# Windowed attention and a soft mixture of experts: groups of 64 queries by eight heads, a masked copy of 32 columns, and the copy of the flipped x on VectorE

## The chip, the cores and the metric

The kernel runs on one core of a Trainium2 chip. The metric is device time in microseconds (us) of one execution. Engines are named as the profile names them: PE is TensorE (PEld its weight loads), DVE is VectorE, ACT is ScalarE, POOL is GpSimd, and SP is the engine that issues most of the transfers. TensorE writes its results into accumulators (the tiles whose names begin with `ps`, `s4`, `pq`, `xp`), which VectorE and ScalarE read; GpSimd works on the core's main memory alone.

## The reference

```python
B, H, S, D = 8, 8, 576, 64
scores = q @ k.T / 8                                   # per batch row and head
rel = pos[:, None] - pos[None, :]
bias = -2.0 ** -(h + 1) * abs(rel)
scores = where((rel >= 0) & (rel < 128), scores + bias, -1e9)
attn = softmax(scores)                                 # over keys
x = (attn @ v) as [B * S, H * D] = [4608, 512]         # all heads of a token side by side
logits = x @ phi                                       # [4608, 32], 8 experts of 4 slots
d = softmax(logits, over tokens); slot_input = d.T @ x # [32, 512]
slot_out[e] = relu(slot_input[e] @ w1[e]) @ w2[e]
out = softmax(logits, over slots) @ slot_out           # [4608, 512]
```

Each query sees its own key and the 127 before it.

## The kernel before

A batch row of 576 queries is cut into tiles of 128 queries, `t` = 0 to 3, and a tail of 64, `t` = 4. A **group** is what goes through the softmax at once: 128 partitions by four pieces of 128 keys. For `t` below 4 a group is 128 queries by four heads (`g` = 0, 1), for `t` = 4 it is 64 queries by eight heads. There are 9 groups a batch row and 72 in all, and the loop `for i in range(n)` (from L777) makes one turn for each.

**Scores** (`scores`, L237). A strip of 32 queries sees a window of 160 keys, five blocks of 32. TensorE first writes the bias ramp into a window of the accumulator with a small product (L259), then adds queries times keys (L266), 8 and 16 products of 32 rows by 160 columns. Tile 0 has no tile before it; there two ramp products (L247) and four products (L252) of 128 by 128 do.

**Masked copy** (`merge`, L274). The window of a strip begins at column 32 r, so that the oldest keys lie in the first 128 columns and the own keys in the second. The copy lays the one over the other under a triangular mask, so that each query has just 128 places: four pieces of 128 by 128 for `t` = 1 to 3 (L281), four of 64 columns for the tail (L283). For tile 0 it writes -1e30 over the keys that are still to come (L279).

**Softmax** (`softmax_front`, L330, and `expo`, L351). On VectorE one turn runs: masked copy of the new group, row maximum (L301), reciprocal of the old group's sums (L313, for which GpSimd's L309 prepares the sums), the scaled maximum (L304), normalisation of the old group (L317). Between them stand "fillers" of the expert routing. ScalarE then takes four exponentials with their sums (L357).

**Values**. Three turns later TensorE flips the attention (`flip`, L372) into the accumulator `pq`, ScalarE copies it out (`split`, L379), and GpSimd selects from it the part for the tile's own keys and the part for the tile before (L381 and L383, for the tail L386 and L388). A turn after that TensorE multiplies with V (`values`, L410): for `t` = 1 to 3 eight products with 128 queries, for tile 0 four, for the tail 16 with 64 queries. The profile shows each product of this precision as two records. ScalarE copies the finished x of a tile out (`x_store`, L426).

**Flipped x**. Each tile of x, two of the rows' tails together, is flipped by TensorE (`x_flip`, L438) into the other half of the banks of `pq`, and copied out (`x_keep`, L447, 128 partitions by 512). Four tiles make a pass: logits (L456), softmax over tokens and slots, and the running sum of slot inputs (L514).

What each engine does is written out by hand in program order: `do` notes an action for a later turn at one of four places (`pre`, `pe`, `act`, `dve`), `run` plays it. `x_flip` is noted for the place `pe`, at the end of a turn, behind the scores of the next group; `x_keep` for the place `act` of the turn after, behind the split and ahead of the product with V. On an engine the order of the program is kept.

After the last group a section written out by hand finishes the last four groups and the routing (L806 to L893, some 213 to 230 us of the span), and then the experts run (from L997): a stream of products with weights that are loaded meanwhile.

Of the kernel before, what the change touches and what calls it, by code (L numbers as in the profile page):

```python
# [23 lines left out]
NS = E * SPE  # L24
# [11 lines left out]
WIN = P + KB  # L36
NB = S // KB
HW = 512
CW = P + TAIL + NS
WARM = 6  # L40
# [28 lines left out]
def tile_attn_softmoe(  # L69
# [20 lines left out]
    mask_u = cst[:, 0:P].bitcast(I32)  # L90
    mask_t = cst[:, P:P + TAIL].bitcast(I32)
# [14 lines left out]
    ramp = cpool.tile([P, 2, 2, WIN], BF16, name="ramp")  # L106
# [4 lines left out]
    qs = [kq[:, NB * P + 2 * P * i:NB * P + 2 * P * i + 2 * P] for i in range(3)]  # L111
# [61 lines left out]
    def load_q(i, eng=None):  # L173
        b, t, g = groups[i]
        o = 4 * P * t + 2 * P * g
        (eng or nc.sync).dma_start(qs[i % 3], qd[b, :, o:o + 2 * P])
# [29 lines left out]
    with tc.manual_schedule(engines=ORDERED):  # L206
# [6 lines left out]
        nc.gpsimd.memset(cst[:, 0:P], 1.0)  # L213
        nc.gpsimd.affine_select(cst[:, 0:P], cst[:, 0:P], [[1, P]], ALU.is_gt, 0.0, base=0, channel_multiplier=-1)
# [17 lines left out]
        nc.scalar.dma_start(cst[:, P:], cstd)  # L232
# [4 lines left out]
    def scores(i):  # L237
        b, t, g = groups[i]
        s4 = s4s[i % 2]
        parts = [s4[:, 0:2], s4[:, 2:4]]  # L240
        if i == 0:
            parts = [ps_1.tile([P, 2, 2 * P], F32, tag="xp", name="s4_0"), pq[:, 0].rearrange("p (u w) -> p u w", u=2)]
            parts = parts[::-1]
        qt = qs[i % 3].rearrange("p (j w) -> p j w", w=width(t))
        if t == 0:
            for par, rows in enumerate(half):
                nc.tensor.matmul(  # L247
                    parts[par][:, :, 0:P], lhsT=ones[rows], rhs=ramp[rows, g, :, 0:P],
                    start=True, stop=False)
            for jj in range(2):  # L250
                for par, rows in enumerate(half):
                    nc.tensor.matmul(  # L252
                        parts[par][:, jj, 0:P], lhsT=qt[rows, jj], rhs=kall[rows, 0:4, 2 * g + jj],
                        start=False, stop=(jj == 1))
        else:
            strips = [(c // 2, c % 2) if t == 4 else (g, c) for c in range(4)]
            for par, rows in enumerate(half):
                for c, (h, r) in enumerate(strips):
                    nc.tensor.matmul(  # L259
                        s4[32 * c:32 * c + 32, 2 * par:2 * par + 2, 32 * r:32 * r + WIN],  # L260
                        lhsT=ones[rows, 0:32], rhs=ramp[rows, h], start=True, stop=False)
            for jj in range(2):
                for par, rows in enumerate(half):
                    for c, (h, r) in enumerate(strips):
                        m0 = 4 * (t - 1) + r
                        nc.tensor.matmul(  # L266
                            s4[32 * c:32 * c + 32, 2 * par + jj, 32 * r:32 * r + WIN],
                            lhsT=qt[rows, 2 * h + jj if t == 4 else jj, 32 * r:32 * r + 32],
                            rhs=kall[rows, m0:m0 + 5, 2 * h + jj], start=False, stop=(jj == 1))
        st[groups[i]] = {"s4": s4, "parts": parts}  # L270

    ALL, LO, HI = slice(0, 4), slice(0, 2), slice(2, 4)

    def merge(key, us=ALL):  # L274
        t = key[1]
        s4 = st[key]["s4"]
        if t == 0:
            m = len(range(4)[us])
            nc.vector.copy_predicated(merged(key, us), bc(mask_u, 1, m), bc(low, 1, m).to_broadcast([P, m, P]))  # L279
        elif t < 4:  # L280
            nc.vector.copy_predicated(s4[:, :, P:2 * P], bc(mask_u, 1, 4), s4[:, :, 0:P])  # L281
# [841 lines left out]
```

## Time and profile before

| | us |
|---|---|
| median of 3 runs (lowest to highest) | 289.14 (288.57 to 290.88) |
| the profiled execution | 288.49 |
| its span, first to last instruction | 286.0 |
| TensorE busy | 253.9 |
| VectorE busy | 221.6 |
| ScalarE busy | 205.6 |
| GpSimd busy | 112.9 |

The prediction's lines are from that one execution. A row of groups gives line, engine, operation, output and inputs, shapes, count, then busy us and mean ns of one, then the idle time of the engine just ahead of them and what ended it. The chain of waits follows the work that ended last back to its releasers; its pieces show start, length, engine, tile, line and, behind x, the records in it. Pieces of a chain are shorter than the rows' means, since one instruction begins before the one ahead of it has quite ended. A row of windows gives the stretch, its length, the busy time (and instructions) of PE, PEld, DVE, ACT and POOL, then the granted clock of TensorE, the share of the transfer engines and GB/s. Matmul ends are modelled, so that a busy TensorE is not one at its peak.

### The profile page before, as it was taken

How to read it: one execution, taken by the hardware profiler on the slowest of the kernel's cores; microseconds unless marked ns; L12 is line 12 of the kernel's file. 1: busy time of each engine (PE TensorE's matmuls, PEld its weight loads, DVE VectorE, ACT ScalarE, POOL GpSimd, SP SyncE). 2: the span in 40 equal slices, each digit the busy share in tenths (PEclk: the TensorE clock that was granted, in tenths of full speed). 3: DMA queues.
4: the chain of work that ended last, by engine and by line, in shares of the span. 5: the costliest groups of instructions: out<-in, count | busy, mean ns of one | idle time of the engine just before them, and what ended most of it. 6: DMA issues, size and time to landing. Idle time of an engine off the chain costs nothing.

```text
span 286.0 us, 13588 instructions
## 1 busy us (share of the span) xinstructions
PE 253.9 (89%) x5535; PEld 178.9 (63%) x5535; DVE 221.6 (77%) x509; ACT 205.6 (72%) x817; POOL 112.9 (39%) x218
## 2 busy tenths in 40 slices
PE   8588999799979889989979998998979899999990
PEld 4366676676757567667657765766756443687750
DVE  2889989998997999988998998798973352656451
ACT  2888889988888988998898988888783411044460
POOL 2044626662573276257527725466552011000000
PEclk9689999999999999999999999999999999999997
DMA  6645368869885987969797978866574579998997
GB/s 184 218 134 164 100 197 270 276 195 289 285 271 152 305 297 233 278 224 305 218 286 242 328 236 251 278 204 219 165 265 140 169 254 365 411 393 322 362 384 282
DMA packets 36754, 72.61 MB, mean 254 GB/s; under 512 B 4402, under 2 KB 15316, under 8 KB 36692
## 3 DMA queue, kind: packets, MB, share of 16 engines
q1 hardware_dynamic: 35972, 71.24, 75.7%
q8 instruction: 43, 0.70, 1.0%
q10 hardware_dynamic: 720, 0.51, 0.6%
q14 instruction: 19, 0.16, 0.2%
HBM read 62.29 MB, written 9.44 MB: 251 GB/s over the span
## 4 chain that ended last, share of the span: by engine, by line
PE 45%; DVE 23%; ACT 16%; POOL 7%; issue 5%; DMA 2%; DVEq 0%; ACTq 0%; POOLq 0%
ACT area L357 9%; PE xp L410 7%; DVE area L317 6%; DVE s L301 6%; PE s L266 5%; PE op L967 5%; PE hp L930 5%; PE po L992 4%; DVE s L281 3%; POOL area L381 3%; PE pq L372 3%; PE lp L456 2%; DVE s L279 2%; PE s L259 2%; ACT area L379 2%
## 5 line engine op out<-in xcount | busy, mean ns | idle before, releaser
L357 ACT ACTIVATE area<-s,nb 128x128 f32<-128x128 f32 x286 | 102.7, 391 | 13.8 <-DVE nb L304 10.4
L410 PE MATMUL xp<-area 128*64 128x128 f32 (+1 forms) x1104 | 74.5, 272 | 8.4 <-POOL area L381 5.3
L357 ACT ACTIVATION_READ_ACCUMULATOR area<-s,nb 128x1 f32 x286 | 65.4, 229 | 0.0
L410 PEld LDWEIGHTS xp<-area 128*64 128x64 f32 x1104 | 54.1, 137 | 18.0 <-POOL area L381 6.1
L317 DVE TENSOR_TENSOR area<-area,rs 128x512 f32<-128x512 f32 (+1 forms) x73 | 61.0, 836 | 1.6
L301 DVE TENSOR_REDUCE s<-s 128x4 f32<-128x512 f32 x71 | 49.5, 697 | 2.2
L379 ACT COPY area<-pq 128x512 f32<-128x512 f32 (+1 forms) x72 | 43.5, 605 | 10.7 <-PE pq L372 9.0
L266 PE MATMUL s<-kq 64*32 64x160 f32 x1792 | 43.8, 302 | 2.3 <-issue 2.3
L309 POOL TENSOR_SCALAR rs<-sm 128x4 f32<-128x4 f32 x70 | 15.0, 214 | 73.0 <-ACT area L357 71.6
L383 POOL TENSOR_SCALAR_AFFINE_SELECT area<-area 128x512 f32<-128x512 f32 x48 | 41.7, 870 | 3.3
L381 POOL TENSOR_SCALAR_AFFINE_SELECT area<-area 128x512 f32<-128x512 f32 x48 | 35.5, 740 | 15.5 <-ACT area L379 14.6
L281 DVE COPY_PREDICATED s<-cst,s 128x512 f32<-128x512 int32 x48 | 33.1, 689 | 6.1 <-PE s L266 5.6
L372 PE MATMUL pq<-unit_r,area 64*128 64x64 f32 x552 | 31.3, 233 | 3.7 <-ACT area L322 2.8
L266 PEld LDWEIGHTS s<-kq 64*32 64x32 f32 x1792 | 30.1, 107 | 4.1 <-issue 3.5
L372 PEld LDWEIGHTS pq<-unit_r,area 64*128 64x128 f32 x552 | 23.3, 140 | 11.8 <-issue 3.2
L259 PE MATMUL s<-ramp,ones 64*32 64x320 bf16 x448 | 18.7, 311 | 4.8 <-ACT area L357 4.5
L426 ACT COPY area<-xp 128x512 f32<-128x512 f32 (+1 forms) x37 | 21.4, 578 | 0.2
L447 ACT COPY area<-pq 128x512 f32<-128x512 f32 x34 | 20.7, 608 | 0.3 <-PE pq L432 0.3
L438 PEld LDWEIGHTS pq<-unit_r,area 64*128 64x128 f32 x264 | 11.1, 137 | 12.8 <-issue 9.7
L994 ACT COPY ob<-po 128x512 f32<-128x512 f32 x19 | 10.4, 591 | 11.4 <-PE po L992 11.4
L994 DVE COPY ob<-po 128x512 f32<-128x512 f32 x17 | 11.2, 686 | 6.6 <-PE po L992 6.5
L438 PE MATMUL pq<-unit_r,area 64*128 64x64 f32 x264 | 15.2, 233 | 0.9 <-ACT area L379 0.6
(173 smaller groups left out, 329.1 us busy)
## 6 DMA issues: line engine op xcount, KB each, us to landing
w<-w SPq DMA_DIRECT2D x53, 512.0 KB, 5.5
out<-ob SPq DMA_DIRECT2D x36, 256.0 KB, 3.9
kq<-q_t SPq DMA_DIRECT2D x69, 128.0 KB, 3.5
kq<-k_t SPq DMA_DIRECT2D x32, 256.0 KB, 3.9
area<-v_n SPq DMA_DIRECT2D x31, 256.0 KB, 4.2
area<-w SPq DMA_DIRECT2D x8, 512.0 KB, 4.6
area<-v_n SPq DMA_DIRECT2D x12, 128.0 KB, 4.4
kq<-w SPq DMA_DIRECT2D x3, 512.0 KB, 5.9
```

What stands on the lines that cost most here:

```text
L259: nc.tensor.matmul(s4[32 * c:32 * c + 32, 2 * par:2 * par + 2, 32 * r:32 * r + WIN], lhsT=ones[rows, 0:32], rhs=ramp[rows, h], start=True, ...
L266: nc.tensor.matmul(s4[32 * c:32 * c + 32, 2 * par + jj, 32 * r:32 * r + WIN], lhsT=qt[rows, 2 * h + jj if t == 4 else jj, 32 * r:32 * r + 32],
L281: nc.vector.copy_predicated(s4[:, :, P:2 * P], bc(mask_u, 1, 4), s4[:, :, 0:P])
L301: nc.vector.tensor_reduce(st[key]["mx"][:, us], merged(key, us), axis=AX.X, op=ALU.max, negate=True)
L317: nc.vector.tensor_tensor(p4, p4, bc(rs, 2, P), op=ALU.mult)
L357: nc.scalar.activation(s["p4"][:, u], merged(key, u), AF.Exp, bias=s["nb"][:, u:u + 1], scale=SCALE, accum_out=s["sm"][:, u:u + 1],)
L372: nc.tensor.transpose(s["pt"][:, u, r], s["p4"][rows, u], ident[rows, rows])
L379: nc.scalar.copy(pa[:, us].rearrange("p u (r w) -> p u r w", r=2), s["pt"][:, us])
L381: nc.gpsimd.affine_select(pp[:, us], pa[:, us], [[0, m], [-1, P]], ALU.is_gt, 0.0, base=0, channel_multiplier=1)
L383: nc.gpsimd.affine_select(pa[:, us], pa[:, us], [[0, m], [1, P]], ALU.is_ge, 0.0, base=0, channel_multiplier=-1)
L410: nc.tensor.matmul(xp[D * par:D * par + D, j, 0:w], lhsT=v_slot[b, t - 1 + ph][:, D * h:D * h + D], rhs=src[:, 2 * par + i] if t < 4 else ...
L438: nc.tensor.transpose(xq[:, j, r], x[rows, j], ident[rows, rows])
```

## The change

A group is now 64 queries by eight heads for every tile. The four strips of 32 partitions are the four pairs of heads; the two heads of a pair (`par`) and the two halves of 32 queries (`uu`) make the four pieces. A pair's two windows lie in one bank, at columns 0 and 224 (`OFF`), so that all strips have their five blocks in the same place. The copy then moves one block of 32 columns a window, in two windows a bank and two banks: 128 elements a partition for every group. Tile 0 gets the same path; its keys before the beginning are closed by four products that add -1e30 (`shut`), and its windows begin later (`skip`).

Each group multiplies all eight heads of 64 queries with V, so that all products have 64 columns: 16 a group, 8 in tile 0. The exponentials of half the pieces write their halves in swapped order, so that the key order of a tile is one. The mask is built by eight selections of GpSimd on 32 partitions each.

`x_keep` is called with VectorE's copy for all tiles but the last one of the loop and those behind it, 32 times. As before it is played at the place `act`, which on VectorE comes behind the normalisation of that turn.

In the section behind the loop the last groups are split and stored by other slices, the last x has a place of its own (`halves(5)`), and one weight load moves behind its flip.

The core of the diff:

```diff
@@ scores
-            strips = [(c // 2, c % 2) if t == 4 else (g, c) for c in range(4)]
+        strips = [slice(KB * c, KB * c + KB) for c in range(NPAIR)]
+        for par, rows in enumerate(half):
+            both = parts[par][:, 0:2 * OFF].rearrange("p (u w) -> p u w", u=2)
+            for c, strip in enumerate(strips):
+                nc.tensor.matmul(
+                    both[strip, :, 0:WIN], lhsT=ones[rows, 0:KB], rhs=bc(ramp[rows, c], 1, 2),
+                    start=True, stop=False)
         if t == 0:
             for par, rows in enumerate(half):
+                for uu in range(2):
+                    r = 2 * g + uu
+                    nc.tensor.matmul(
+                        parts[par][:, OFF * uu:OFF * uu + WIN], lhsT=ones[rows], rhs=shut[rows, KB * r:KB * r + WIN],
+                        start=False, stop=False)
+        for uu in range(2):
+            r = 2 * g + uu
+            skip = max(4 * (1 - t) - r, 0)
+            m0 = 4 * (t - 1) + r
+            for par, rows in enumerate(half):
+                for c, strip in enumerate(strips):
+                    nc.tensor.matmul(
+                        parts[par][strip, OFF * uu + KB * skip:OFF * uu + WIN], lhsT=qt[rows, c, uu],
+                        rhs=kall[rows, m0 + skip:m0 + 5, c], start=False, stop=(uu == 1))
@@ merge
-            nc.vector.copy_predicated(s4[:, :, P:2 * P], bc(mask_u, 1, 4), s4[:, :, 0:P])
+        x = windows(key, us).rearrange("p a (x y) -> p a x y", y=KB)
+        m = x.shape[1]
+        nc.vector.copy_predicated(
+            x[:, :, 0:12:11, :], bc(mask.bitcast(I32), 1, m), x[:, :, 4:8:3, :])
@@ values
-                        xp[D * par:D * par + D, j, 0:w], lhsT=v_slot[b, t - 1 + ph][:, D * h:D * h + D],
+                        xp[D * par:D * par + D, j, TAIL * g:TAIL * g + TAIL],
+                        lhsT=v_slot[b, t - 1 + ph][:, D * h:D * h + D], rhs=(pp, pd)[ph][:, :, par, j],
@@ after_values
         if (b, t) != tiles[-1]:
-            do("act", turn[0] + 1, x_keep, b, t)
+            do("act", turn[0] + 1, x_keep, b, t, nc.vector.tensor_copy)
@@ behind the loop
-            load_weight()
         x_flip(last, 4, pq[:, 1])
         x_flip(last, 0, free[1])
+        load_weight()
```

The change moves instructions in two places on which the prediction rests. The first is VectorE in a turn of the second batch row, with the semaphores that each row waits for. Before, from a masked copy (L281) to the next:

```order
L281 COPY_PREDICATED s_0_83<-cst,s_0_83 128x4x128 [waits PE_49]
L301 TENSOR_REDUCE s_0_83<-s_0_83 128x4 [waits DVE_49]
L313 RECIPROCAL rs<-rs 128x4 [waits Pool_49]
L304 TENSOR_SCALAR nb<-s_0_83 128x4 [waits DVE_49]
L317 TENSOR_TENSOR area<-area,rs 128x512 [waits DVE_49,Activation_49]
L281 COPY_PREDICATED s_1_84<-cst,s_1_84 128x4x128 [waits PE_49]
```

and now, from one masked copy (L285) to the next, with the copy of the flipped x (L451):

```order
L285 COPY_PREDICATED s_1_84<-cst,s_1_84 128x2x2x32 [waits PE_49]
L301 TENSOR_REDUCE s_1_84<-s_1_84 128x2x2 [waits DVE_49]
L314 RECIPROCAL rs<-rs 128x4 [waits Pool_49]
L305 TENSOR_SCALAR nb<-s_1_84 128x4 [waits DVE_49]
L318 TENSOR_TENSOR area<-area,rs 128x512 [waits DVE_49,Activation_49]
L451 COPY area<-pq 128x512 [waits Activation_49]
L285 COPY_PREDICATED s_0_83<-cst,s_0_83 128x2x2x32 [waits PE_49]
```

The masked copy shrank from 4 x 128 to 2 x 2 x 32, and the copy out of `pq` stands between the normalisation and the next masked copy, waiting for ScalarE. On ScalarE the split (L385) of the turn behind it waits for VectorE:

```order
L385 COPY area<-pq 128x512 [waits PE_49]
L364 ACTIVATE area,sm<-s_0_83,nb 128x128 [waits DVE_49,Pool_49]
L364 ACTIVATE area,sm<-s_0_83,nb 128x128 x3
L385 COPY area<-pq 128x512 [waits DVE_49,PE_49]
L430 COPY area<-xp 128x512 [waits PE_49]
```

The first split waits for TensorE alone, the second for VectorE's copy as well; in the kernel before, the splits stand on the engine of that copy itself.

The second place is TensorE in the loop, from the product with V of one group to the flips of the next. Before, at a tile 0 (L247 and L252 are its scores):

```order
L410 MATMUL xp<-area 64x128 x8
L247 LDWEIGHTS ones
L247 MATMUL s_1_84<-ramp,ones 128x2x128
L247 LDWEIGHTS ones
L247 MATMUL s_1_84<-ramp,ones 128x2x128
L252 MATMUL s_1_84<-kq 128x128 x4
L372 MATMUL pq<-unit_r,area 128x64 x8
```

and now, the scores of the tile 0 of the same batch row from the products of the closed keys (L265) on:

```order
L265 LDWEIGHTS ones
L265 MATMUL s_1_84<-cst,ones 128x160
...
L274 MATMUL s_1_84<-kq 32x32 x8
L274 MATMUL s_1_84<-kq 32x64 x8
L379 MATMUL pq<-unit_r,area 128x64 x8
L411 MATMUL xp<-area 64x64 x16
```

Eight ramp products (L258) stand ahead of these rows. Four wide products (the rows left out are three more like the first two) and 16 narrow ones stand where two ramp products and four of 128 by 128 stood, and the product with V has 16 instructions of 64 columns where it had eight of 128.

More of the change, by code (lines that the diff above doesn't have):

```diff
@@ L105, in tile_attn_softmoe @@
     kq = cpool.tile([P, 3 * UW], F32, name="kq")
-    ramp = cpool.tile([P, 2, 2, WIN], BF16, name="ramp")
+    ramp = cpool.tile([P, NPAIR, WIN], BF16, name="ramp")
     ones = cpool.tile([P, P], BF16, name="ones")
@@ L212, in tile_attn_softmoe @@
         nc.vector.memset(fine[:, 10:11], -1.0)
-        nc.gpsimd.memset(cst[:, 0:P], 1.0)
-        nc.gpsimd.affine_select(cst[:, 0:P], cst[:, 0:P], [[1, P]], ALU.is_gt, 0.0, base=0, channel_multiplier=-1)
+        nc.gpsimd.memset(shut, 0.0)
+        for par in range(2):
+            nc.gpsimd.memset(shut[64 * par:64 * par + 1, 0:P], LOW)
+        nc.gpsimd.memset(mask, 1.0)
+        for c in range(4):
+            rows = slice(KB * c, KB * c + KB)
+            nc.gpsimd.affine_select(
+                mask[rows, 0], mask[rows, 0], [[-1, KB]], ALU.is_ge, 0.0, base=0, channel_multiplier=1)
+            nc.gpsimd.affine_select(
+                mask[rows, 1], mask[rows, 1], [[1, KB]], ALU.is_gt, 0.0, base=0, channel_multiplier=-1)
         load_k(0, 0)
@@ L238, in scores @@
         b, t, g = groups[i]
-        s4 = s4s[i % 2]
-        parts = [s4[:, 0:2], s4[:, 2:4]]
         if i == 0:
-            parts = [ps_1.tile([P, 2, 2 * P], F32, tag="xp", name="s4_0"), pq[:, 0].rearrange("p (u w) -> p u w", u=2)]
-            parts = parts[::-1]
-        qt = qs[i % 3].rearrange("p (j w) -> p j w", w=width(t))
+            parts = [pq[:, 0], ps_1.tile([P, 2 * QB], F32, tag="xp", name="s4_0")]
+        else:
+            parts = [s4s[i % 2][:, 2 * par:2 * par + 2].rearrange("p u w -> p (u w)") for par in range(2)]
@@ L262, in scores @@
[L262 to L269, printed above, removed]
@@ L296, in rowmax, with windows @@
+        m = x.shape[1]
+        nc.vector.copy_predicated(
+            x[:, :, 0:12:11, :], bc(mask.bitcast(I32), 1, m), x[:, :, 4:8:3, :])
+    def windows(key, us):
+        if number[key] == 0:
+            return st[key]["parts"][us.start // 2].unsqueeze(1)
+        return st[key]["s4"]
+    def merged(key, us):
+        x = windows(key, us).rearrange("p a (u w) -> p a u w", u=2)
+        return x[:, :, :, 0:P]
     def rowmax(key, us):
-        if "mx" not in st[key]:
-            o = P - merged_at(key)
-            st[key]["mx"] = st[key]["s4"][:, :, o] if number[key] else work.tile([P, 4], F32, tag="mx", name="mx")
+        if "nb" not in st[key]:
```

131 lines of the change are left out of this document (54 added, 77 removed).

## The prediction

> **What bounds the kernel now.** I read the whole execution first, then its chain of waits, then two stretches of the table of windows.
>
> ```profile
> PE 253.9 (89%) x5535; PEld 178.9 (63%) x5535; DVE 221.6 (77%) x509; ACT 205.6 (72%) x817; POOL 112.9 (39%) x218
> PE 45%; DVE 23%; ACT 16%; POOL 7%; issue 5%; DMA 2%; DVEq 0%; ACTq 0%; POOLq 0%
> ACT area L357 9%; PE xp L410 7%; DVE area L317 6%; DVE s L301 6%; PE s L266 5%; PE op L967 5%; PE hp L930 5%; PE po L992 4%; DVE s L281 3%; POOL area L381 3%; PE pq L372 3%; PE lp L456 2%; DVE s L279 2%; PE s L259 2%; ACT area L379 2%
> 140.00:165.00 25.00, 23.47 (x622) 17.51 (x614) 23.93 (x53) 23.00 (x97) 13.98 (x26) 1.00 0.88 272
> 210.00:220.00 10.00, 7.86 (x102) 5.68 (x104) 4.43 (x15) 5.83 (x22) 3.82 (x8) 1.00 0.62 215
> 220.00:230.00 10.00, 8.62 (x68) 5.15 (x64) 3.48 (x11) 3.44 (x9) 0.92 (x3) 1.00 0.66 215
> 230.00:286.00 56.00, 48.19 (x742) 30.09 (x741) 26.84 (x68) 15.65 (x32) 1.82 (x5) 0.97 0.92 345
> ```
>
> The window rows give length, then busy time of TensorE, its weight loads, VectorE, ScalarE and GpSimd. The kernel has two parts. From 230 us on it is the expert part, where only TensorE is busy; the change does not touch it. In the attention part, about 205 us, three engines are busy for 92 to 96% of the stretch shown, so no single one is the bound: the chain changes hands. VectorE holds 23% of 286, or 66 us, nearly all of it here. TensorE holds 45%, 129 us; L967, L930 and L992 (14%, 40 us) are the expert part, and in the lead-in to it, 210 to 230 us, TensorE is busy for 16.5 us: about 70 us are left. So each of the two carries about a third of the attention part, and ScalarE and GpSimd most of the rest.
>
> **The masked copy.** Its three forms, the smallest operation of VectorE in each turn, and the two rows nearest to the moved copy:
>
> ```profile
> L281 DVE COPY_PREDICATED s<-cst,s 128x512 f32<-128x512 int32 x48 | 33.1, 689 | 6.1 <-PE s L266 5.6
> L279 DVE COPY_PREDICATED s<-cst,fine 128x512 f32<-128x512 int32 x15 | 14.9, 997 | 0.1
> L283 DVE COPY_PREDICATED s<-cst,s 128x256 f32<-128x256 int32 x8 | 3.4, 422 | 0.3 <-PE s L266 0.3
> L304 DVE TENSOR_SCALAR nb<-s 128x4 f32<-128x4 f32 x71 | 10.7, 151 | 0.1
> L447 ACT COPY area<-pq 128x512 f32<-128x512 f32 x34 | 20.7, 608 | 0.3 <-PE pq L432 0.3
> L424 DVE COPY area<-xp 128x512 f32<-128x512 f32 x1 | 0.7, 677 | 0.0
> ```
>
> Now each group copies two slots of 32 columns in two windows, 128 elements a partition. From 512 to 256 elements the row falls by 267 ns; another 128 fewer take off 134, which gives an estimate of 288 ns. It cannot be above the 256-element row (422). Below, the 151 ns of L304 are the floor. Of L281's 3% of the chain (8.6 us), (689-288)/689 goes, 5.0 us; of L279's 2% (5.7 us), (997-288)/997 goes, 4.1 us. **Term 1: -9.1 us**, between -6.6 (at 422 ns) and -11.5 (at 151).
>
> **The copy of the flipped x** leaves ScalarE 32 times. It stood on the chain in eight pieces, 3.3 us together, the first and the last:
>
> ```profile
> 41.35 0.59 ACT area L447
> 168.19 0.14 ACT area L447
> ```
>
> **Term 2: -3.3 us**; at worst 0, if the next thing ScalarE waits for ends at the same time. On VectorE each costs about 0.68 us (the 677 ns row, also out of TensorE's accumulators), 21.8 us of busy time. VectorE is the chain for about a third of the attention part (66 of 205, less a few us of the expert part), so of 21.8 I take 0.31: **term 3: +6.7 us**. The bounds are 0, if every copy falls where VectorE waits for scores anyway (5.6 us of such waits in L281's row), and 21.8. VectorE's busy time as a whole falls: 48 x 0.40 + 15 x 0.71 + 8 x 0.13 = 31 us go, 21.8 come.
>
> **TensorE gets more.** Pieces of the chain, start and length:
>
> ```profile
> 60.28 0.25 PE pq L372 x8
> 60.53 1.02 PE xp L410 x16
> 61.55 0.26 PE s L259 x8
> 61.81 0.54 PE s L266 x32
> 62.35 0.39 PE pq L372 x8
> 62.75 1.08 PE xp L410 x32
> 134.68 0.22 PE s L247 x2
> 134.90 0.47 PE s L252 x8
> ```
>
> The product with V has twice the instructions of half the width. The last tile of each batch row has that form already: 1.08 us for 32 records against 1.02 for 16. So 48 groups gain 0.06 us each, 2.9 us. For tiles 1 to 4 the scores keep their 8 + 32 records. For tile 0 (16 groups) they were 0.22 + 0.47 = 0.69 us. They become 8 ramp products (0.26), 4 wide products for the closed keys, and 16 products of 32 to 128 columns. The four wide ones have the shape of L247 with less than half the width each: 0.22 at least. The narrow ones take between half of 0.54 (their mean width is 80 of 160) and all of it. Between a ramp and a wide product the shape of the weights changes, and back; eight flips cost 0.39 behind scores and 0.25 behind other flips, so a change of shape may cost 0.14, twice. The group costs 0.75 to 1.52 instead of 0.69. I take +0.45, since the narrow products still bring 32 weight loads (near the 0.54 row) while the wide ones are at their lower end: 7.2 us for 16 (1.0 to 13.3). With the 2.9 that is 10.1 us, a third of it on the chain: **term 4: +3.3 us** (1.3 if the low end, 16.2 if all of it counts at the high end).
>
> **A wait that is new.** The copy reads the banks into which the next attention flips are written. The order of the changed program shows that the copy waits for ScalarE, whose split reads the same banks, and that ScalarE's next split waits for VectorE; the flips of the next turn wait for the copy too. Before, the copy stood behind the split on ScalarE itself.
>
> ```profile
> 72.13 0.61 DVE s L281
> 72.77 0.70 DVE s L301
> 73.47 0.08 DVE rs L313
> 73.54 0.06 DVE nb L304
> 73.60 0.04 issue
> 73.65 1.09 DVE area L317
> 76.25 0.74 DVE area L317
> PEld pq L372 <- ACT area L447: 1.0, 3, 0.4
> DVE rs L313 <- POOL rs L309: 3.2, 10, 0.5
> ```
>
> From the end of a group's scores VectorE now needs 0.29 + 0.70 + 0.08 + 0.06 + 0.04 (the gap behind them) + 0.74 for the normalisation + 0.68 for the copy, 2.6 us. In that time TensorE does x flips 0.25, flips 0.39, values 1.08 and the next scores 0.80, 2.5 us, and stands before the flips that need the copied bank. So a flip waits 0.1 us when all goes well, and 0.5 when the normalisation takes 1.09 rather than 0.74, or when the reciprocal waits for GpSimd (up to 0.5 in the last row). What is queued behind those flips is the product with V and the next scores, for which VectorE waits in turn. 32 x 0.1 x 1/3 is **term 5: +1.1 us**, between 0 and 32 x 0.5 = 16. [...]
>
> Terms at nothing: GpSimd has the same number of selections of the same size; the twelve small set-up operations have until the first masked copy, which waits for the first scores; one weight load moves behind the flips of the last x, where TensorE, not loads, is the chain; if that cover were gone it would cost the 0.6 us that these flips last.
>
> **Sum**, from the profiled execution's 288.49 us (span 286.0 and 2.5 around it): -9.1 - 3.3 + 6.7 + 3.3 + 1.1 = -1.3, so 287.2. The median of the runs is 289.14, 0.65 above the profiled one: **287.8 us**.
>
> **Rivals.** *The relief goes through.* The copies fill VectorE's waits for scores (term 3 is 0), flips never wait (term 5 is 0), and half of TensorE's addition falls into its own waits: -9.1 - 3.3 + 1.7 = -10.7, so 278.4 in terms of the median. For it: VectorE and ScalarE both get slack, and TensorE is busy 94% where busy includes the tails of its pipeline. Against it: three engines at 92 to 96% leave little that is nobody's chain.
>
> *The flips wait for the copy* (the other side). TensorE is held at the first flip behind each of the 32 copies for 0.5 us, 16 us; this contains the copy's own time on the chain, so term 3 drops out: -9.1 - 3.3 + 3.3 + 16 = +6.9, so 296.0. It decides from the point where VectorE starts a turn some 0.4 us late, as it does wherever the normalisation runs at 1.09. Against it: the shorter masked copy gives 0.4 us a turn back.
>
> *Tile 0 is dear.* At the high end, all on the path, TensorE gains 16.2 us while the copies are hidden: -9.1 - 3.3 + 16.2 = +3.8, so 292.9. Against it: where tile 0's scores run, VectorE was the later one (L279 at 997 ns).
>
> That the masked copy gets no cheaper is excluded by its size; that it stays at 422 ns moves the sum by 2.5 us, within the forecast's own range.
>
> **Chances.** The forecast has 0.43, with its own range 284 to 291.5 (terms 1 to 3 at their nearer bounds). The relief has 0.27, the waiting flips 0.22, tile 0 0.08. A measurement of this kernel tells about 1%, 2.9 us, from no change: faster is below 286.2, slower above 292.0. Faster: 0.27 and 0.12 of the forecast's, 0.39. Slower: 0.22, 0.05 of tile 0's, 0.01 of the forecast's, 0.28. The rest, 0.33, is within 1%. The range from 279 to 296 leaves out the outer half of the two large rivals.
>
> **What would show it.** Right: a masked copy near 0.29 us; VectorE's share of the chain smaller and TensorE's larger; V products of 1.08 us for 32 records; tile 0's scores near 1.1 us; flips that idle on VectorE's copy for about 0.1 us in most of 32 turns. The relief would show as a VectorE that waits for scores in nearly every turn and an attention part of about 195 us. The waiting flips would show as several us of TensorE idle before flips, with the VectorE copy as releaser. The forecast is wrong if the attention part changes by more than 4 us either way.

## The result, and the profile after

The changed kernel takes 305.0 us (median of four runs, 302.7 to 313.5), the kernel before in the same job 289.6 us. The ratio is 1.050, 95% interval 1.039 to 1.062: slower by 5%, some 14.6 us. Here and below, a median counts every run, but a ratio leaves out the executions that fell into a slower state (here the one of 313.5 us), so the two need not agree. The forecast of 287.8 us, a little faster than before, was wrong in its direction and by more than its range allowed.

The page of the profiled execution (span 301.0 us) answers line by line to the one of before:

```profile
PE 263.1 (87%) x6975; PEld 190.4 (63%) x6975; DVE 213.1 (71%) x541; ACT 195.2 (65%) x785; POOL 120.6 (40%) x228
q8 instruction: 55, 0.90, 1.2%
PE 65%; DVE 12%; issue 8%; ACT 5%; POOL 4%; DMA 2%; SPq 0%; DVEq 0%; POOLq 0%; ACTq 0%
PE xp L411 16%; PE s L274 9%; PE pq L379 6%; DVE area L318 5%; PE op L971 5%; PE hp L934 5%; PE s L258 4%; ACT area L364 4%; PE po L996 3%; PE pq L442 3%; DVE area L451 2%; PE lp L460 2%; PE ap L518 2%; POOL area L392 2%; DVE s L301 2%
L285 DVE COPY_PREDICATED s<-cst,s 128x128 f32<-128x128 int32 x71 | 20.6, 291 | 23.7 <-PE s L274 23.1
L451 DVE COPY area<-pq 128x512 f32<-128x512 f32 x32 | 21.9, 684 | 1.6 <-ACT area L385 1.5
```

TensorE's share of the chain went from 45 to 65%, VectorE's from 23 to 12, and the time named issue from 5 to 8. VectorE's and ScalarE's busy time fell, as the change intends, but VectorE now waits 23.1 us for scores. The second line is a queue that the prediction did not look at: the one that carries instructions. It moved 55 blocks, 0.90 MB. The same line of before:

```profile
q8 instruction: 43, 0.70, 1.0%
```

The count fits TensorE's row of the page. In the trace each of these transfers has 16,384 bytes. Before, 43 blocks stand beside 5535 recorded products and as many weight loads, which makes 63.6 bytes for each record; now 55 blocks stand beside 6975 of each, 64.6 bytes. So a block holds about 128 recorded products with their weight loads (129 before, 127 now), and this change makes TensorE read a quarter more code.

Both kernels split cleanly at the first product of the experts, at 231.1 us before and at 246.5 us now. The table of windows, from 8 us to that point and from there to the end; the columns are the stretch, its length, then busy time of TensorE, its weight loads, VectorE, ScalarE and GpSimd, the granted clock, and the transfers' share and rate. Before:

```profile
8.00:231.00 223.00, 200.69 (x4736) 146.53 (x4736) 192.29 (x433) 188.40 (x781) 109.37 (x203) 0.98 0.74 233
231.00:286.00 55.00, 47.31 (x735) 29.18 (x734) 26.51 (x67) 14.89 (x30) 1.82 (x5) 0.97 0.92 345
```

and now:

```profile
8.00:246.40 238.40, 209.98 (x6108) 158.48 (x6108) 184.03 (x464) 177.57 (x747) 115.19 (x203) 0.98 0.70 217
246.40:301.00 54.60, 47.32 (x735) 29.18 (x734) 26.52 (x67) 14.90 (x30) 1.82 (x5) 0.98 0.93 355
```

The whole loss is in the attention part, 15.4 us: TensorE is busy 9.3 us longer and idle 6.1 us longer. (The two profiled executions show it; the 14.6 us above are from all runs.) What TensorE waits for from 8 us to 232 us, before (the largest rows: what waited, for whom, us in total, times, longest):

```profile
PE xp L410 <- POOL area L381: 5.3, 6, 1.4
PE s L259 <- ACT area L357: 4.5, 9, 1.3
PE pq L372 <- ACT area L322: 2.8, 1, 2.8
PE s L266 <- issue: 2.3, 4, 1.0
```

and now:

```profile
PE xp L411 <- issue: 6.3, 5, 2.1
PE pq L379 <- DVE area L451: 4.8, 8, 1.1
PE s L274 <- issue: 4.7, 5, 1.5
...
PE pq L379 <- issue: 1.6, 2, 0.9
PE pq L442 <- DVE area L451: 1.2, 2, 0.9
```

Over the whole of the two attention parts, the waits for GpSimd fell from 6.6 to 0.2 us and those for ScalarE from 10.3 to 7.1. Two kinds took their place: 6.0 us for VectorE's copy, which the prediction had named, and waits for nothing that a semaphore shows (named issue), 13.3 us in 13 pieces instead of 2.3 in 4. Three of these, in the timeline of TensorE (start, length, and in brackets the idle time before the row):

```profile
63.06 0.51 PE L274 MATMUL s<-kq 64*32 64x160 f32 x16 [1.36 <-issue]
...
127.06 0.27 PE L411 MATMUL xp<-area 128*64 128x64 f32 x2 [1.34 <-issue]
...
169.94 0.45 PE L411 MATMUL xp<-area 128*64 128x64 f32 x7 [2.14 <-issue]
```

They interrupt a run of like products. In the trace's record of transfers, blocks of code landed at 61.72, 125.61 and 168.63 us: TensorE resumed 1.34, 1.45 and 1.31 us later. It is so with all 13 pieces: each ends 1.28 to 1.54 us after the landing of a block. Over the 19 profiled executions of this document, the attention parts hold 161 waits of TensorE named issue, and all 161 end 1.20 to 1.63 us after the last block's landing. Of the 412 other waits there, a tenth does, about what chance gives with a block every 4 to 5 us. So these are waits for code. That gives the theory to test, and its rivals:

- **Supply.** The change gives TensorE a quarter more code; blocks that come through transfer engines which are 70% busy come late, and TensorE stands.
- **Copy.** VectorE's copy, behind a normalisation of 0.87 us, holds the flips.
- **Work.** The additional products cost their own time, with or without anything else.
- **Relief.** What VectorE and ScalarE lose is worth the terms 1 and 2 of the forecast.

### The profile page after: what moved, and what is told of

It reads as the page before. It is cut to its first block, busy times and chain, and to the rows that moved or that the text cites. A ratio compares the mean times of both kernels' runs of the same rounds, so it can differ in the third digit from the quotient of the medians.

```text
span 301.0 us, 16459 instructions
## 1 busy us (share of the span) xinstructions
PE 263.1 (87%) x6975; PEld 190.4 (63%) x6975; DVE 213.1 (71%) x541; ACT 195.2 (65%) x785; POOL 120.6 (40%) x228
## 4 chain that ended last, share of the span: by engine, by line
PE 65%; DVE 12%; issue 8%; ACT 5%; POOL 4%; DMA 2%; SPq 0%; DVEq 0%; POOLq 0%; ACTq 0%
PE xp L411 16%; PE s L274 9%; PE pq L379 6%; DVE area L318 5%; PE op L971 5%; PE hp L934 5%; PE s L258 4%; ACT area L364 4%; PE po L996 3%; PE pq L442 3%; DVE area L451 2%; PE lp L460 2%; PE ap L518 2%; POOL area L392 2%; DVE s L301 2%
## 5 line engine op out<-in xcount | busy, mean ns | idle before, releaser
L411 PE MATMUL xp<-area 128*64 128x64 f32 x1984 | 76.7, 228 | 6.8 <-issue 6.3
L411 PEld LDWEIGHTS xp<-area 128*64 128x64 f32 x1984 | 66.0, 140 | 12.6 <-issue 7.6
L385 ACT COPY area<-pq 128x512 f32<-128x512 f32 (+1 forms) x72 | 42.2, 588 | 30.3 <-PE pq L379 19.9
L390 POOL TENSOR_SCALAR_AFFINE_SELECT area<-area 128x512 f32<-128x512 f32 (+1 forms) x57 | 47.9, 841 | 34.3 <-ACT area L385 31.3
L274 PE MATMUL s<-kq 64*32 64x160 f32 (+4 forms) x2288 | 53.6, 292 | 4.7 <-issue 4.7
L301 DVE TENSOR_REDUCE s<-s 128x4 f32<-128x512 f32 (+1 forms) x72 | 50.0, 694 | 2.2
L392 POOL TENSOR_SCALAR_AFFINE_SELECT area<-area 128x512 f32<-128x512 f32 (+1 forms) x57 | 48.6, 853 | 3.9
L274 PEld LDWEIGHTS s<-kq 64*32 64x32 f32 x2288 | 35.5, 108 | 7.6 <-issue 4.5
L285 DVE COPY_PREDICATED s<-cst,s 128x128 f32<-128x128 int32 (+1 forms) x72 | 20.9, 290 | 23.7 <-PE s L274 23.1
L430 ACT COPY area<-xp 128x512 f32<-128x512 f32 (+1 forms) x37 | 20.3, 549 | 14.6 <-PE xp L411 14.2
L258 PE MATMUL s<-ramp,ones 64*32 64x320 bf16 x572 | 24.7, 313 | 3.9 <-ACT area L364 2.1
L451 DVE COPY area<-pq 128x512 f32<-128x512 f32 x32 | 21.9, 684 | 1.6 <-ACT area L385 1.5
L314 DVE RECIPROCAL rs<-rs 128x4 f32<-128x4 f32 (+1 forms) x73 | 12.5, 171 | 9.2 <-POOL rs L310 8.8
```

The costliest lines, as they stand in the source:

```text
L258: nc.tensor.matmul(both[strip, :, 0:WIN], lhsT=ones[rows, 0:KB], rhs=bc(ramp[rows, c], 1, 2), start=True, stop=False)
L274: nc.tensor.matmul(parts[par][strip, OFF * uu + KB * skip:OFF * uu + WIN], lhsT=qt[rows, c, uu], rhs=kall[rows, m0 + skip:m0 + 5, c], star ...
L301: nc.vector.tensor_reduce(st[key]["mx"], merged(key, us), axis=AX.X, op=ALU.max, negate=True)
L385: nc.scalar.copy(pa[:, us].rearrange("p u (r w) -> p u r w", r=2), s["pt"][:, us])
L390: nc.gpsimd.affine_select(prev, own, [[-KB, m], [0, 8], [-1, KB]], ALU.is_gt, 0.0, base=-i0, channel_multiplier=1)
L392: nc.gpsimd.affine_select(own, own, [[KB, m], [0, 8], [1, KB]], ALU.is_ge, 0.0, base=i0, channel_multiplier=-1)
```

## The experiments

Times are medians; the ratio is to the kernel before on the same chip in the same job, with its 95% interval. Where a ratio is turned into us, it is multiplied by 289.6. Waits are those of one profiled execution of each kernel.

### The copy back on ScalarE

```diff
-            do("act", turn[0] + 1, x_keep, b, t, nc.vector.tensor_copy)
+            do("act", turn[0] + 1, x_keep, b, t)
```

> The changed kernel with the copy of the flipped x back on ScalarE; all else stays. The copy theory: TensorE's 6.0 us of waits on VectorE's copy (4.8 before the flips of the weights, 1.2 before the flips of x) go, and the time falls from 305.0 to 299 to 301 us. Its rival, that the place of the copy doesn't matter because other waits of the same length follow: 304 to 306 us. The relief theory, by which VectorE's room was worth something and ScalarE's 0.59 us per copy would come back onto the chain: 306 us or more. The supply theory speaks of none of this: TensorE's waits named issue stay near 13 us.

Measured: 305.5 us, 1.052 (1.041 to 1.064). Nothing is won. By itself this spoke for the rival: the edit takes away what caused the 6.0 us of waits on VectorE's copy, and the time stays.

### The copy ahead of the normalisation

```diff
-        normalise(old, HI if first else ALL)
+        if first or number[new] <= SKIP:
+            normalise(old, HI if first else ALL)
...
             run("act", i)
+            if i > max(1, SKIP):
+                normalise(groups[i - 1], ALL)
```

> The changed kernel, the copy still on VectorE, but written ahead of the normalisation of the same step instead of behind it. The normalisation takes 0.87 to 1.20 us, so each copy ends about 1 us earlier. The copy theory: TensorE's waits on the copy (6.0 us) fall to under 2 us and the time to 300 to 302 us. The rival, that it is VectorE's 0.68 us for each copy that costs, wherever it stands: 304 to 306 us, as the changed kernel.

Measured: 306.6 us, 1.060 (1.052 to 1.068). The largest waits of TensorE, from 8 to 220 us, and the one row on the copy that is left:

```profile
PE s L274 <- issue: 6.4, 5, 2.2
PE xp L412 <- issue: 5.1, 3, 1.9
...
PE pq L380 <- DVE area L452: 0.5, 1, 0.5
```

The edit did what it should: the waits on the copy fell from 6.0 to 0.5 us. The time did not follow. The waits for code are 14.9 us in sum instead of 13.3, and TensorE's busy time is 267.6 us instead of 263.1. At least a part of the latter is its clock: between 20 and 250 us it was granted at half in four pieces of 3.4 us, each during a wait for code or within about 2 us behind it, where the changed kernel's execution had two such pieces (last section). Two more can cost 3.4 us, an estimate from their 6.8 us at half the clock. So the copy theory is right about the wait and wrong about its worth here: what was won went to later code and a lower clock, and this run can't part the two.

### Ramps and closed keys in two products

```diff
-            for c, strip in enumerate(strips):
-                nc.tensor.matmul(
-                    both[strip, :, 0:WIN], lhsT=ones[rows, 0:KB], rhs=bc(ramp[rows, c], 1, 2),
-                    start=True, stop=False)
-        if t == 0:
...
+            nc.tensor.matmul(
+                both[:, :, 0:WIN], lhsT=ones[rows], rhs=ramp[rows, 0 if t else 1 + g], start=True, stop=False)
```

> The changed kernel with the bias ramps of a group in two products of 64x128 by 320 columns (a selector matrix picks the row of the head) instead of eight of 64x32, and tile 0's closed keys folded into the same two; the scores come out the same, and TensorE's program falls from 4936 to 3944 instructions, near the 3976 of before. The supply theory: waits named issue fall from 13.3 us to 2 to 5 us, and the time from 305.0 to 294 to 298 us. The work theory: what falls is the products' own time alone, 4 products of tile 0 in each of 16 groups (about 0.25 us each time, 4.0 us), against a change of shape in the other 55 groups that may take 0.1 us each; 301 to 307 us, with the waits named issue as they were.

Measured: 304.1 us, 1.052 (1.040 to 1.063); waits named issue 7.2 us. The code shrank less than I had counted: a ramp product is one record where a score product is two (8 records for eight ramps, 32 for 16 scores), so the page has 6479 products, 51 blocks, not the 43 of before. The waits for code fell by almost half, but the wide products cost time of their own: in the trace the ramps take 0.24 us before the scores start, instead of 0.14, in 56 groups, and the scores behind them 0.05 us more, some 8 us together, against 4.3 saved in tile 0. The run is inconclusive: it trades one cost for another of the same size.

### The kernel before with split products of the values

```diff
-                    nc.tensor.matmul(
-                        xp[D * par:D * par + D, j, 0:w], lhsT=v_slot[b, t - 1 + ph][:, D * h:D * h + D],
...
+                    for o in range(0, w, TAIL):
+                        nc.tensor.matmul(
+                            xp[D * par:D * par + D, j, o:o + TAIL], lhsT=v_slot[b, t - 1 + ph][:, D * h:D * h + D],
```

> The kernel before with each product of the values that is 128 columns wide split in two of 64 columns, as the changed kernel has them; nothing else is changed. TensorE's program grows from 3976 to 4424 instructions. The work theory: 0.06 us in each of 48 groups, 2.9 us at most, so 289.6 to 292.5 us, and waits named issue near 2.3 us. The supply theory: in proportion to the instructions added (448 of the 960 of the change) 4 to 6 us of further issue waits, 293 to 298 us in all.

Measured: 300.0 us, 1.039 (1.032 to 1.045). This single part, which adds 896 recorded products and no new work, makes the old kernel 11 us slower; the expectation had 2.9 for the products themselves. Its rows (queue of instructions; share of the chain by engine):

```profile
q8 instruction: 50, 0.82, 1.1%
PE 60%; DVE 14%; ACT 11%; issue 6%; POOL 4%; DMA 2%; DVEq 0%; ACTq 0%; POOLq 0%
```

Seven blocks more than before, 8.0 us of waits named issue instead of 2.3, and TensorE takes over the chain, as in the changed kernel. It came out slower than even the supply theory had asked for.

### One weight block for all: the changed kernel, and before

```diff
         m, e, k = units[n]
+        if n:
+            wt[units[n]] = wt[units[0]]
+            return
```

> The changed kernel with only the first weight block loaded and used in place of all 64 (63 loads of 512 KB are left out, so the experts compute with wrong weights); the program of every engine but SyncE is as it was. To be read in the attention part alone, which ends at about 228 us; the expert part gets faster because its loads are gone. The supply theory, now with the row that the queue of instructions carries 55 blocks of 16384 B where TensorE's page has 6975 products (128 a block): a block that shares the transfer engines with less data comes sooner, so the waits named issue, 13.3 us before 226 us, fall to under 6 us and the attention part by 6 to 9 us. Its rival, a fixed cost for each block whatever else is moved: issue waits stay at 11 to 15 us and the attention part changes by less than 2 us. The work theory: no change either.

> The kernel before with only the first weight block loaded and used in place of all 64 (wrong weights in the experts); the partner of the run on the changed kernel. Attention part of before: about 213 us, with 2.3 us of issue waits on TensorE. The supply theory: little to win, since VectorE and GpSimd hold the flips and values; 0 to 4 us less in the attention part. If traffic slows the engines themselves (shorter copies or products), both kernels win alike.

Measured: the changed kernel 292.6 us, 1.011 (1.006 to 1.017); the kernel before 287.9 us, 0.993 (0.989 to 0.996). These kernels leave out 63 of the 64 loads of weights, so the experts work with one block's numbers throughout. The four engines that compute have as many instructions as with all loads, and the blocks of code stay 55 and 44 (43 with all loads); yet 11.3 us go from the one and 2.2 from the other. The changed kernel's attention part and, of its waits up to 220 us, those for the copy and the two largest named issue:

```profile
8.00:236.50 228.50, 207.14 (x6108) 156.11 (x6108) 186.57 (x472) 176.24 (x747) 116.38 (x204) 0.99 0.42 125
```

```profile
PE pq L382 <- DVE area L454: 6.8, 11, 1.2
...
PE pq L445 <- DVE area L454: 2.3, 4, 1.1
...
PE lp L463 <- issue: 1.4, 2, 0.8
PE s L277 <- issue: 0.8, 2, 0.5
```

With the transfers at 0.42 instead of 0.70, the attention part is 228.5 us long instead of 238.4, and the waits for code are 2.8 us in all instead of 13.3. The waits for VectorE's copy grew instead, from 6.0 to 9.1 us. The rival that each block has a fixed cost falls: the same 55 blocks cost little when little else is moved. That traffic slows the engines themselves falls too as the main cause, since the same loads cost the kernel before only 2.2 us.

### Split values with one weight block

> The kernel before with the products of the values split in halves of 64 columns and, besides, only the first weight block loaded (the experts compute with wrong weights). With all weights the split took 300.0 us against 289.2, and without them the unsplit kernel 287.9. The supply theory: nearly all of the split's 10.7 us is stalls of code that arrives late beside the weights, so without these loads only the products' own 2.9 us is left: 289 to 291.5 us. The work theory: the split costs its 10 us with or without the loads: 296 to 300 us.

Measured: 290.6 us, 1.004 (1.001 to 1.006). Against the unsplit kernel without the loads (0.993) the split costs 1.1%, 3.2 us, where it cost 11 with the loads. The term of 2.9 us that the prediction had for it was right for the products; the other 8 us belong to the loads beside them.

### Copy on ScalarE with one weight block

> The changed kernel with one weight block in place of all (wrong weights in the experts) and the copy of the flipped x back on ScalarE. With the weights left out and the copy on VectorE it took 292.6 us, and TensorE waited 9.1 us on that copy. The copy theory, in the form that is left after the runs in which the copy was moved and nothing was won: the wait is real but hidden behind late code, so once code comes in time moving the copy is worth something: 288 to 290.5 us. Its rival, that other waits follow at once: 291.5 to 293.5 us.

Measured: 288.4 us, 0.996 (0.993 to 1.000). Without the loads, moving the copy is worth 1.5%, 4.3 us; with them it was worth nothing. That settles most of the puzzle of the first two runs: the wait was real, and taking it out gains where code comes in time.

### The copy on VectorE in the kernel before

> The kernel before with the copy of the flipped x on VectorE behind the normalisation; nothing else of the change. VectorE, which is busy 185.8 of 204 us there, gets 32 copies of 0.68 us, 21.8 us, and ScalarE loses 18.9 us. The third and fifth terms of the forecast together: 4.5 us (3.3 off, 6.7 and 1.1 on), 292 to 296 us. If VectorE is full: up to 21.8 us, 300 to 311 us. If TensorE sets the floor of this kernel too: 289 to 291 us.

Measured: 296.5 us, 1.026 (1.019 to 1.032), 7.4 us, at the upper end of what the forecast's own terms gave. How it costs, in the kernel's largest waits of TensorE:

```profile
PE pq L372 <- DVE area L447: 13.6, 14, 1.7
PE pq L438 <- DVE area L447: 5.6, 7, 1.4
```

21 waits of 0.9 us, not 32 of 0.1. Here code is in time (waits named issue 1.4 us), and the chain shows who sets the end:

```profile
DVE 45%; PE 40%; ACT 4%; POOL 4%; issue 4%; DVEq 0%; ACTq 0%; POOLq 0%
```

VectorE, 23% of the chain before, has 45 now. I read its additional time and the flips' wait for it as the same thing seen from two sides.

### Before without masked copies

```diff
     def merge(key, us=ALL):
+        if number[key]:
+            return
```

> The kernel before without the masked copies of all groups but the first (the scores stay unmasked there, so the result is not the reference's): VectorE loses about 29 us of 221.6. It tells what relief on VectorE is worth at most. The relief theory of the forecast, by which a copy's saved time on VectorE's share of the chain goes through: the chain names VectorE for 23 percent, so some 10 to 20 us fall, 270 to 280 us. The theory that TensorE's stream sets the floor: TensorE is busy 184.7 of the 204 us from 8 to 212, so at most some 5 us, 284 to 289 us, with new waits named issue on TensorE.

Measured: 283.2 us, 0.976 (0.968 to 0.983), 7.0 us faster. VectorE's busy time fell from 221.6 to 175.5 us (the 29 us in the expectation was too low). So even leaving out the masked copies of all groups but the first, 46 us of VectorE, buys 7. The relief theory asked for 10 to 20.

### Tile 0 alone with folded ramps, with all weights and with one

```diff
+            for strip in strips if t else [slice(0, P)]:
+                nc.tensor.matmul(
+                    both[strip, :, 0:WIN], lhsT=ones[rows, strip], rhs=ramp[rows, 0 if t else 1 + g],
+                    start=True, stop=False)
```

> The changed kernel with the ramps and the closed keys of tile 0 alone (16 of 72 groups) in two products of 64x128 by 320 columns instead of eight of 64x32 and four of 64x128; the other groups keep their eight. The scores come out the same. TensorE's program: 4616 instructions instead of 4936. In the trace the ramps and closed keys of tile 0 took 0.26 and 0.25 us, where two wide products in the run with all ramps in two took 0.24 us together, against 0.05 us more for the scores behind them: 0.22 us in each of 16 groups, 3.5 us. The work theory: 301 to 302 us. The supply theory: 160 products are 1.3 blocks fewer, 1 to 2 us more of gain, 299 to 301 us. If the wait of the flips takes the room: 304 to 306 us.

> The changed kernel with one weight block in place of all (wrong weights in the experts) and the ramps and closed keys of tile 0 in two wide products. The partner with one weight block took 292.6 us. The work theory of tile 0: 0.22 us in each of 16 groups, 3.5 us, 288.5 to 290 us. If the waits for the copy on VectorE, 9.1 us in the partner, take the room: 291.5 to 293 us.

Measured: with all weights 306.2 us, 1.042 (1.030 to 1.054), within the spread of the changed kernel; with one weight 288.3 us, 1.002 (0.998 to 1.006), 0.95% or 2.8 us below the partner's 1.011, give or take 2 us by the two intervals. It fits the pattern: what is taken off TensorE has a worth where code comes in time, and none that can be told where it doesn't.

### What in the loads holds the code up

Three edits of the weight loads: each as two loads of half the columns; the halves in different groups; every second load left out.

```diff
-        nc.sync.dma_start(wt[units[n]], (w1d, w2d)[m][e, :, UW * k:UW * (k + 1)])
+        for o in range(0, UW, 512):
+            nc.sync.dma_start(wt[units[n]][:, o:o + 512], (w1d, w2d)[m][e, :, UW * k + o:UW * k + o + 512])
```

> The changed kernel with each weight load of 512 KB made as two loads of 256 KB, by columns, so that a row of a transfer is 2 KB instead of 4 KB; the same bytes and the same work otherwise. If a code block waits for a number of rows that stand ahead of it, it waits half as long: waits named issue fall from 13.3 us to 7 to 9 us and the time to 298 to 302 us. If it waits for bytes, or for the data of the transfer before: 303 to 307 us, as the changed kernel.

> The changed kernel with each weight load of 512 KB made as two of 256 KB that are issued in different groups of queries as far as 72 halves over 54 groups allow, so that the same bytes come in shorter bunches. If what holds the code up is that a bunch of some 5 us stands ahead of it: issue waits fall from 13.3 us to 7 to 10 us, 299 to 302 us. If it is the share of the transfer engines that the loads take over the whole attention part: 303 to 307 us, as the changed kernel.

> The changed kernel with every second weight load left out and the block before used in its place (the experts compute with wrong weights). The changed kernel took 305.0 us with 64 loads and 292.6 with one. If the code is held up in proportion to the bytes: halfway, 297 to 300 us, with 6 to 9 us of issue waits. If only a nearly full transfer system holds it up: 292 to 295 us.

Measured: 304.7 us, 1.054 (1.047 to 1.061), waits named issue 12.7 us; 300.9 us, 1.039 (1.030 to 1.048), 12.2 us; 303.7 us, 1.050 (1.043 to 1.058), 6.6 us. Rows of half the length changed nothing that these runs can tell (304.7 us against 305.0). Spread halves may help a little, but the intervals overlap with the changed kernel's. Half of the loads halve the waits for code, as the theory in bytes has it (the transfers' share of the attention part fell from 0.70 to 0.58), and yet the time does not move at all. VectorE's copy is waited for longer instead, 11.1 us:

```profile
PE pq L382 <- DVE area L454: 6.6, 8, 2.0
PE pq L445 <- DVE area L454: 4.5, 5, 1.8
```

The clock adds to it: this execution had 10.2 us at half clock between 20 us and the experts, the changed kernel's 6.8. So the waits for code alone don't account for all that the loads cost, and how the cost grows with the loads is not settled.

### Spread loads on the kernel before, and three repairs together

> The kernel before with its weight loads of 512 KB made as halves of 256 KB, issued in different groups as far as they go. All of the loads cost this kernel 1.9 us (289.8 against 287.9 with one). The supply theory: at most that can be won, 288 to 290 us. If shorter bunches help the data of the groups as well (q, k and v come sooner): 285 to 287.5 us.

> The changed kernel with the copy back on ScalarE, tile 0's ramps and closed keys in two wide products, and the weight loads in spread halves, all weights loaded. Without the loads, the copy was worth 4.2 us and tile 0 4.3 us; if both went through, 292 us from the 300.9 of the spread loads. The supply theory: every wait that is taken out makes the code due sooner, as when the copy was moved with the loads in place and nothing was won, so most of it is lost again: 296 to 301 us. Slower than before in both cases.

Measured: 290.5 us, 1.003 (0.998 to 1.008); and 301.8 us, 1.045 (1.037 to 1.052), with 10.6 us of waits named issue. The spread gains nothing where code isn't late. Copy, tile 0 and spread together stay where the spread alone was, just above the 296 to 301 us of the supply theory: the 7.1 us that the first two are worth without the loads are swallowed. No version that does the whole work is faster than the kernel before.

The table that carries the verdict. Blocks are those of the queue of instructions; the cost of the loads is the difference of the two ratios:

| kernel | blocks | with all loads | with one load | cost of the loads |
|---|---|---|---|---|
| before | 43 | 1 | 0.993 | 2.2 us |
| before, values split | 50 | 1.039 | 1.004 | 10.2 us |
| changed, tile 0 folded | 53 | 1.042 | 1.002 | 11.7 us |
| changed | 55 | 1.050 | 1.011 | 11.3 us |
| changed, copy on ScalarE | 55 | 1.052 | 0.996 | 16.2 us |

The same loads cost 2 us in a kernel with 43 blocks and 10 to 16 with 50 and more. By the intervals of the two ratios, the first cost is good to 1 us, the second to 2 and the other three to about 4, so that these three can't be told apart. The work theory has no room for the step from 2 to 10 and more, the relief and copy theories neither.

## Why the prediction was wrong, point by point

**The missing term** is the largest, and the step that failed: among the "terms at nothing" there is none for the code that TensorE reads. The prediction counted what each new product takes, "The product with V has twice the instructions of half the width", and priced it by a row of 1.08 us against 1.02. That row is from a tile where code was in time. It never asked what carries the instructions, though q8 stood on the page. The loads cost the changed kernel 11.3 us and the kernel before 2.2: 9.1 us that no term and no rival had.

**"So each of the two carries about a third of the attention part."** This reading let two thirds of TensorE's additions fall into nobody's time. TensorE was busy 200.7 of 223.0 us there, with the least slack of all. Without the loads, the split of the values costs 3.2 us, all of the 2.9 that its rows give, and the fold of tile 0 wins 2.8 us of the 4.3 that its rows give (0.26 + 0.25 less 0.24 us in 16 groups). Together that is 6.0 us; **term 4** had 3.3 of 10.1. Its prices were near: values 1.08 us, as in the chain below, tile 0's scores 0.26 + 0.25 + 0.54 = 1.05 us against the 1.1 that the list had asked for (the 1.52 of its upper end holds the wide products at 0.44, which the text does not say). The factor of a third was the error.

```profile
82.77 1.08 PE xp L411 x32
83.86 0.26 PE s L258 x8
84.11 0.25 PE s L265 x4
84.36 0.54 PE s L274 x32
```

**Term 1**, the masked copy: 291 ns, forecast 288. The price was right; its worth was not. The forecast credited the copy's share of the chain in full, 9.1 us. Leaving out all masked copies but the first in the kernel before gave 7.0. In the changed kernel without loads, what remains of 5.4 us (1.011 less 0.993) after 4.3 for the copy, 3.2 for the values and 2.8 for tile 0 is -4.9 us, which I put to the masked copies by subtraction. That number is argued, not measured by itself; it carries the errors of four runs, and the part of tile 0's addition that the fold does not take back (0.09 us in 16 groups, 1.4 us) is in it as well. A share of the chain says what was last, not what falls when it goes: without the masked copies, TensorE's share of the kernel before rose from 45 to 58%.

**Terms 2, 3 and 5**, the move of the copy: +4.5 us together in the forecast; measured +7.4 in the kernel before and +4.3 in the changed kernel without loads. The size held roughly (two pieces of half clock, up to 3.4 us, are in the 7.4); that the two can be priced apart did not: VectorE's time (term 3) reaches the end through the flips that wait for it (term 5), and that wait is 21 times 0.9 us in the kernel before and 9.1 us in the changed one without loads, not 32 times 0.1. The working of term 5 let VectorE start a turn with the end of the scores; a normalisation of 1.20 us, as in the rows that follow, alone takes 0.46 us more than the 0.74 that it used. The wait is where the prediction put it, before flips into the bank that the copy reads (0.26 us in the rows that follow, 6.0 us in 10 waits in the whole of the changed kernel's attention part). No run shows the 0.1 us in each of 32 turns that term 5 was worked out from; the runs showed fewer and longer waits in its place.

```profile
80.21 1.20 DVE L318 TENSOR_TENSOR area<-area,rs 128x512 f32<-128x512 f32 x1
...
81.33 0.68 DVE L451 COPY area<-pq 128x512 f32<-128x512 f32 x1
...
82.07 0.46 PE L442 MATMUL pq<-unit_r,area 64*128 64x64 f32 x8 [0.26 <-DVE area L451]
```

**The sum.** -4.9 for the masked copies, +4.3 for the copy, +6.0 for TensorE's products, +9.1 for code that comes late: +14.5, against 14.6 measured. This has to come out so, since the first number is a remainder and the last is the loads' cost of 11.3 us in this kernel less the 2.2 before: the sum orders the loss and proves none of its parts.

**The rivals.** *The flips wait* was nearest in time (296.0 us) and named a wait that was there, 6.0 us in the changed kernel; but with all loads, taking the wait out gained nothing. *Tile 0 is dear* fell. So did *the relief goes through*: VectorE did wait for scores, 23.1 us, but the attention part grew. Of the list of what would show it, the masked copy, the shares of the chain, the values and tile 0's scores came as listed; the flips idled on the copy 10 times for 0.6 us, not in most of 32 turns for 0.1; and the last line decided: the attention part changed by 15 us, not by less than 4.

**Open**: by which property the loads hold code up, and why their cost is more than the waits named issue in some kernels (split values: 10.2 us, of which the waits fell by 5.9, from 8.0 to 2.1). The clock can be a part of it in the changed kernel (6.8 us at half clock with all loads, none with one, up to 3.4 us), not with split values, which had none in either.

## What to carry to other kernels

Count instructions as a resource, with the bytes of code that TensorE reads beside the bytes of data: twice as many products of half the width cost 3 us where the transfer engines were 43% busy and 11 us where they were 70% busy. Before crediting relief on one engine, look at how much slack the next one has in the same stretch, and test the credit by leaving the operation out altogether. And when an experiment that removes a wait gains nothing, repeat it with the other suspect taken away, since a cost that another one hides looks like none.

## What the runs showed of the hardware that was not expected

- TensorE's code arrived in blocks of 16,384 bytes, one for about 128 recorded products with their weight loads, and where a block was late TensorE resumed 1.20 to 1.63 us after it had landed, 161 times of 161.
- By the trace's clock records, TensorE's granted clock fell to half in pieces of 3.4 us in the midst of the attention part: at 155 and 213 us in the changed kernel's profiled run, where stalls of 0.68 and 1.45 us had just ended; four times with the copy ahead; never in the kernel before. A piece of 3.4 us can cost up to 1.7 us, an estimate from its length at half the clock. The 19 profiled executions have 22 such drops between 20 us and the experts, two of them of 6.8 us, all during a wait of TensorE of 0.7 to 2.7 us or within about 2 us behind it: 18 waits for code, three for VectorE's copy, one for ScalarE. So late code is not the only wait that goes with them, and not every wait is followed by one: with the spread halves a wait for code of 2.2 us was not. That the waits bring them on is likely from the order of events and was not tested; it would be part of what the loads cost beyond the waits. The row of the clock in tenths over 40 slices of the span, changed and with the copy ahead:

```profile
PEclk9799999999999999999989999999799999999998
```

```profile
PEclk9799997999999999999979997999799999999996
```

- Fewer products were not shorter: from the start of the ramps to the start of the scores, two wide products took 0.24 us where eight narrow ones of the scores' own shape took 0.14. That the change of shape between the products is the reason was not tested.
